# Ten more matmuls of zeros ahead of two groups of transposes in an attention and MLP kernel

## The chip, the cores and the metric

The kernel runs on one core of a Trainium2 chip. The metric is the device time of one execution in microseconds; the time of a kernel is the median of several executions. A profile is one more execution, recorded instruction by instruction. Engines are named as in the profile: PE (TensorE's matmuls), PEld (its weight loads), DVE (VectorE), ACT (ScalarE), POOL (GpSimd) and SP (SyncE).

## The reference

For each of 8 batches there are 8 heads with 512 tokens `x` and 32 states `state`, 64 wide. Tokens read the states and states read the tokens with a softmax each way; the 544 rows of a batch, 512 wide over the heads, then go through a two-layer MLP of width 2048 with a leaky activation of its own slope per unit.

```python
scores = scale * np.matmul(x, state.transpose(0, 1, 3, 2))       # softmax over the 32 states
xread = np.matmul(a, state)
scores2 = scale * np.matmul(state, x.transpose(0, 1, 3, 2))      # softmax over the 512 tokens
sread = np.matmul(a2, x)
attn_out = np.concatenate([xread, sread], axis=2)
h = attn_out_rows @ w_in                                         # 4352 x 512 @ 512 x 2048
g = np.maximum(h, 0.0) + alpha * np.minimum(h, 0.0)
out = g @ w_out
```

## The kernel before

All work is cut into steps, and the text `ORDER` (from line 17) lists the steps of the whole kernel in the order in which they are issued. The loop over `ORDER` (line 799) splits each entry at the dots and calls the function of that name. An engine takes its instructions in that order and waits at each for what it needs; nothing is rearranged behind it. So for each engine the order in `ORDER` is the order of its queue.

The steps that matter around the change, for batch 0:

- `lx0`, `lst`, `wi`, `wo`, `lx`: transfers issued by POOL's queue. `lx0` (line 202) brings the second half of the heads of x, `lst` (line 218) the states of batches 1 to 7, `wi.0` (line 224) the first quarter of w_in. The first half of x and the states of batch 0 come by the queues of SP and ACT and are cast by `xc` and `stc`.
- `stt.0`, `sto`: transposes of the states of batch 0 on PE, into PSUM bank 0, and their copy by ACT.
- `xt.b.j.g.k` (line 308): four transposes on PE of 128x128 parts of x, for the half `g` of the heads, into bank `k`. `xo` (line 315) copies them to `xT`, on the engine that its last letter names. `xt.0.1.1.3` and `xt.0.0.1.4` read what `lx0` brought.
- `sc.0.0` and `sc.0.1` (line 318): the scores of the first and the second half of the heads, eight small matmuls each, into the double bank `two`. `sc.0` computes all sixteen again, for the softmax of the tokens.
- `sb.0.0`, `smax.0.0`, `ssh.p.0.0`, `sexp.0.0` and so on: the softmax of a half, on DVE, DVE, POOL and ACT.
- `str.i.k` (line 286): fourteen transposes on PE of half of the states that `lst` brought, into bank `k`; `sro` (line 291) copies them on ACT. `str.0.5` uses bank 5, `str.1.0` bank 0.
- `m.b.f.k0.k1`: the product of the states of batch `b` with a quarter `f` of w_in; `mo` casts it out of PSUM. `m.0.0.1.2` needs `wi.0`.
- `Z.k.n`: `zeros(k, n)` (line 240), `n` matmuls of a constant tile of zeros with itself into bank `k`. Nothing reads what they write. Before the change there are 76 of them, all in the first 17 us.

`single(k, ...)` (line 157) takes bank `k` of PSUM; a step that writes a bank waits until the one before has been written and read.

Of the kernel before, what the change touches and what calls it, by code (L numbers as in the profile page):

```python
# [15 lines left out]

ORDER = """
lx0 id lst stc xc.1.v xc.0.a oma wi.0 lx.1 Z.1.20 stt.0 Z.2.9 xt.0.1.0.1 xt.0.0.0.2 xo.0.1.0.v
xo.0.0.0.v sto.a Z.0.7 sc.0.0 xt.0.1.1.3 xt.0.0.1.4 str.0.5 sb.0.0 xo.0.0.1.v xo.0.1.1.a Z.1.4
sc.0.1 smax.0.0 str.1.0 sro.0.a wi.1 sb.0.1 wo.0 smax.0.1 wi.2 ssh.p.0.0 sro.1.a sexp.0.0 Z.1.3 sc.0  # L20
m.0.0.1.2 ssh.p.0.1 mo.0.0.a.0 Z.5.5 m.1.0.3.4 m.2.0.5.0 tm.0 mo.2.0.a.0 ssum.0.0 sexp.0.1
mo.1.0.a.0 mo.2.0.a.1 wo.1 Z.1.12 m.3.0.1.5 Z.3.7 xt.1.1.0.3 snorm.p.0.0 mo.1.0.v.1 te.0.1
# [809 lines left out]
```

## Time and profile before

| | us |
|---|---|
| median of three runs | 209.64 |
| lowest and highest of the three | 209.15, 209.68 |
| the profiled execution | 209.78 |
| its span, from the first to the last instruction | 208.0 |

| engine | busy us | share of the span | instructions |
|---|---|---|---|
| PE | 200.0 | 96% | 2028 |
| DVE | 175.3 | 84% | 273 |
| ACT | 145.5 | 70% | 291 |
| POOL | 181.0 | 87% | 119 |

Times in the timelines count from the start of the span. A timeline row has the start, the length of the merged group, the engine, the line, the operation, the tile written and the tiles read, the count, and in brackets the idle time of the engine before the group and what ended it. A matmul's length holds its way through the array, so matmuls overlap; how far apart they start is what they cost. The chain of waits is followed back from the last instruction: at each step to what released it, or to the instruction before it on its engine.

### The profile page before, as it was taken

The page shows a single profiled execution, that of the slowest core. Times are in us where ns is not written, and L with a number is a line of the kernel's source. Part 1 is how long each engine was busy: PE and PEld are TensorE (multiplying, and loading weights), DVE is VectorE, ACT ScalarE, POOL GpSimd, SP SyncE. Part 2 cuts the span into 40 slices and gives each one's busy share as a digit, 9 for nine tenths or more (in the row PEclk, how much of TensorE's full clock was granted, in tenths as well). Part 3 has the DMA queues.
Part 4 walks back from the last instruction along what each step waited for, and adds up shares of the span by engine and source line. Part 5 has one row for each costly group of instructions (what it writes and reads, how often), then busy time and mean ns, then how long its engine had stood idle before and what let it go on. Part 6 is the DMA issues. An engine that isn't in the chain of part 4 may idle for free.

```text
span 208.0 us, 5125 instructions
## 1 busy us (share of the span) xinstructions
PE 200.0 (96%) x2028; PEld 135.2 (65%) x2028; DVE 175.3 (84%) x273; ACT 145.5 (70%) x291; POOL 181.0 (87%) x119
## 2 busy tenths in 40 slices
PE   7789999999999999999999999999999999999993
PEld 6553344346557775766677776666678777888892
DVE  1797998999999999999999999998995997754331
ACT  4398996699998899988889579778654645451210
POOL 7569958999999999998999999979996972969960
PEclk9999999999999999999999999999999999999999
DMA  6999999799996749999995166035401144134143
GB/s 154 177 203 208 205 203 160 95 128 194 223 184 87 125 55 225 201 132 156 185 235 87 44 147 167 21 84 151 104 0 54 18 83 154 32 65 159 50 156 101
DMA packets 44792, 27.11 MB, mean 130 GB/s; under 512 B 22096, under 2 KB 42464, under 8 KB 44768
## 3 DMA queue, kind: packets, MB, share of 16 engines
q0 software_dynamic: 14192, 12.03, 38.3%
q1 hardware_dynamic: 29872, 14.23, 29.8%
q10 hardware_dynamic: 704, 0.52, 0.8%
q8 instruction: 16, 0.26, 0.5%
q14 instruction: 8, 0.07, 0.1%
HBM read 17.31 MB, written 8.91 MB: 126 GB/s over the span
## 4 chain that ended last, share of the span: by engine, by line
PE 71%; DVE 14%; ACT 5%; DMA 4%; POOL 4%; issue 2%; POOLq 0%
PE p L667 41%; PE h L518 19%; DVE gp L568 8%; DMA w_in_sb<-in_moe_w_in_dram 4%; PE h L527 3%; PE m_ps L485 3%; PE sr_ps L460 2%; ACT m L507 1%; DVE aT L396 1%; ACT neg L550 1%; DVE m L507 1%; POOL s L644 1%; ACT e L423 1%; POOL an L386 1%; PE o L587 1%
## 5 line engine op out<-in xcount | busy, mean ns | idle before, releaser
L550 ACT ACTIVATE neg<-h 128x512 f32<-128x512 f32 (+1 forms) x144 | 78.5, 583 | 27.4 <-PE h L518 18.5
L568 DVE SCALAR_TENSOR_TENSOR gp<-neg,oma_sb,h 128x512 f16<-128x512 f32 x128 | 89.0, 735 | 6.8 <-ACT neg L550 6.4
L518 PE MATMUL h<-aT,m 128*128 128x512 f16 x250 | 68.6, 379 | 0.3 <-DVE gp L568 0.3
L644 POOL TENSOR_TENSOR s<-gp,s 128x1024 f16<-128x1024 f16 x28 | 65.8, 2398 | 1.2 <-DVE gp L568 0.6
L667 PEld LDWEIGHTS <-gp 128*128 128x128 f16 x432 | 41.7, 98 | 13.9 <-issue 1.9
L667 PEld LDWEIGHTS <-s 128*128 128x128 f16 x368 | 35.2, 98 | 12.7 <-POOL s L644 1.7
L667 PE MATMUL p<-ws,s 128*128 128x256 f16 x248 | 37.3, 273 | 0.2 <-POOL s L644 0.2
L644 POOL TENSOR_TENSOR s<-gp 128x1024 f16<-128x1024 f16 x14 | 31.6, 2265 | 6.5 <-DVE gp L568 6.4
L518 PEld LDWEIGHTS <-m 128*128 128x128 f16 x250 | 23.6, 98 | 16.1 <-issue 3.3
L667 PE MATMUL p<-ws,gp 128*128 128x256 f16 x224 | 33.6, 273 | 0.0
L507 ACT CAST m<-m_ps 128x512 f16<-128x512 f32 x51 | 28.8, 599 | 4.8 <-PE m_ps L485 3.4
L667 PE MATMUL p<-w_out_sb,gp 128*128 128x256 f16 x208 | 30.6, 273 | 0.0
L370 POOL TENSOR_TENSOR ts<-ts,mx 128x1024 f32<-128x1024 f32 (+1 forms) x9 | 17.2, 1909 | 5.7 <-DVE mx L364 5.7
L667 PE MATMUL p<-w_out_sb,s 128*128 128x256 f16 x120 | 18.3, 273 | 0.0
L386 POOL TENSOR_TENSOR an<-ts,r 128x1024 f16<-128x1024 f32 (+1 forms) x9 | 16.3, 1810 | 1.8 <-DVE r L381 1.8
L587 PE MATMUL o<-w_out_sb,gp 128*128 128x512 f16 x64 | 16.6, 379 | 0.1
L620 POOL DMA_DIRECT2D gp<-gp x14 | 13.2, 967 | 3.5 <-issue 2.9
L568 DVE SCALAR_TENSOR_TENSOR gs<-neg,oma_sb,h 128x256 f16<-128x256 f32 x16 | 7.2, 478 | 8.2 <-ACT neg L550 8.2
L485 PE MATMUL m_ps<-w_in_sb,stT 64*32 64x512 f16 x256 | 11.7, 383 | 0.3
L587 PEld LDWEIGHTS <-gp 128*128 128x128 f16 x64 | 5.9, 97 | 8.1 <-issue 1.3
L423 ACT ACTIVATE e<-sc,nb 128x512 f16<-128x512 f32 x16 | 11.1, 694 | 0.1
L698 ACT COPY p<-p 128x512 f32<-128x512 f32 x11 | 6.5, 588 | 6.4 <-PE p L667 6.4
(76 smaller groups left out, 248.9 us busy)
## 6 DMA issues: line engine op xcount, KB each, us to landing
out_dram<-c SPq DMA_DIRECT2D x27, 256.0 KB, 3.1
xg<-in_x_dram POOLq DMA_DIRECT2D x7, 512.0 KB, 8.1
gp<-gp POOLq DMA_DIRECT2D x14, 256.0 KB, 3.6
w_in_sb<-in_moe_w_in_dram POOLq DMA_DIRECT2D x4, 512.0 KB, 11.8
w_out_sb<-in_moe_w_out_dram POOLq DMA_DIRECT2D x4, 512.0 KB, 13.1
out_dram<-osb SPq DMA_DIRECT2D x4, 256.0 KB, 4.4
out_dram<-c SPq DMA_DIRECT2D x3, 128.0 KB, 2.2
x<-in_x_dram SPq DMA_DIRECT2D x1, 256.0 KB, 3.3
```

The source lines that it names most:

```text
L370: engine(e).tensor_tensor(ts, ts, over_blocks(cols(live["mx", b], j, S // N)), ALU.subtract)
L386: engine(e).tensor_tensor(blocks(cols(live["an", b], j, S)), blocks(cols(live["ts", b], j, S)), over_blocks(cols(live["r1", b], j, S // N) ...
L423: nc.scalar.activation(live["e2", b][:, g, :, :], live["sc", b][:, :, :, g, :].rearrange("p r j s -> p (r j) s"), EXP, bias=live["nb", b][ ...
L485: nc.tensor.matmul(t[N * k : N * (k + 1), :], st_head(b, h)[64 * r : 64 * r + 64, :], w_in_sb[64 * r : 64 * r + 64, c, 512 * f : 512 * (f ...
L507: copier(e)(m_tile(b)[:, f, g, :], live["mp", b, f][g])
L518: nc.tensor.matmul(h.rearrange("p (r j s) -> p r j s", r=2, j=2), ms[b][:, f, g, 128 * j : 128 * (j + 1)], weights(b, g), start=(g == 0), ...
L550: nc.scalar.activation(neg, h, RELU, bias=0.0, scale=-1.0)
L568: nc.vector.scalar_tensor_tensor(gt, negs.pop((b, jc)), oma_sb[:, jc : jc + 1], h, ALU.mult, ALU.add)
L587: nc.tensor.matmul(outs[b, q], token_cols(b, jc, q), w_out_sb[:, jc, :], start=(jc == 0), stop=(jc == n_jc - 1),)
L620: nc.gpsimd.dma_start(gp[:, 1, 0], gp[:, 1, 1], accum_op=ALU.add)
L644: engine(e).tensor_tensor(t, x, y, op)
L667: nc.tensor.matmul(chains[chain][:, t, :], lhs, rhs[:, i, :], start=(opens and i == 0 and t == 0), stop=(i == half_k - 1), skip_group_chec ...
```

## The change

Two entries are put into `ORDER`. `Z.0.6`, six matmuls of zeros into bank 0, stands behind `sc.0.0` and ahead of `xt.0.1.1.3`. `Z.0.4`, four of them, stands behind `xt.0.0.1.4` and ahead of `str.0.5`. The order of all other steps is kept.

```diff
 lx0 id lst stc xc.1.v xc.0.a oma wi.0 lx.1 Z.1.20 stt.0 Z.2.9 xt.0.1.0.1 xt.0.0.0.2 xo.0.1.0.v
-xo.0.0.0.v sto.a Z.0.7 sc.0.0 xt.0.1.1.3 xt.0.0.1.4 str.0.5 sb.0.0 xo.0.0.1.v xo.0.1.1.a Z.1.4
+xo.0.0.0.v sto.a Z.0.7 sc.0.0 Z.0.6 xt.0.1.1.3 xt.0.0.1.4 Z.0.4 str.0.5 sb.0.0 xo.0.0.1.v xo.0.1.1.a Z.1.4
 sc.0.1 smax.0.0 str.1.0 sro.0.a wi.1 sb.0.1 wo.0 smax.0.1 wi.2 ssh.p.0.0 sro.1.a sexp.0.0 Z.1.3 sc.0
```

## The prediction

> **What bounds the kernel now.** I read the page's first two parts, then the chain of waits over the first 62 us, then each engine's timeline around the two places where zeros are put.
>
> ```profile
> span 208.0 us, 5125 instructions
> ...
> PE 200.0 (96%) x2028; PEld 135.2 (65%) x2028; DVE 175.3 (84%) x273; ACT 145.5 (70%) x291; POOL 181.0 (87%) x119
> ...
> PEclk9999999999999999999999999999999999999999
> ```
>
> PE is busy 96% of the span, so ten more matmuls look like a cost. But that is a mean over stages. Both groups of zeros fall between 7 and 9 us, and what counts is what sets the end there. The chain of waits, from its window over the start (start us, us, what):
>
> ```profile
> 2.81 0.54 POOL st L219
> 3.35 7.87 DMA w_in_sb<-in_moe_w_in_dram
> 11.22 0.04 issue
> 11.27 0.41 PE m_ps L485 x8
> 11.68 0.39 PE z L244 x5
> 12.06 0.57 PE m_ps L485 x16
> 12.63 0.02 issue
> 12.65 0.59 ACT m L507
> ```
>
> From 3.35 to 11.22 us the end is set by one transfer, the first quarter of w_in. PE joins the chain only at 11.27, with the states' first products (m.0.0 of the order). Whatever PE does before that is free as long as it is ready by then. PE's timeline up to there (start us, us, engine, line, operation, tiles, count, idle time before and its releaser):
>
> ```profile
> 1.10 2.31 PE L244 MATMUL z<-zero 128*128 128x128 f16 x20 [1.10 <-DVE zero L238]
> ...
> 5.78 0.55 PE L244 MATMUL z<-zero 128*128 128x128 f16 x7
> 6.95 0.30 PE L325 MATMUL sc<-xT,stT 64*32 64x256 f16 x8 [0.61 <-DVE xT L316]
> 7.49 0.62 PE L311 MATMUL xT_ps<-ident,xg 128*128 128x128 f16 x8 [0.24 <-DMA xg<-in_x_dram]
> 8.72 0.58 PE L259 MATMUL st_ps<-ident,st 128*64 128x128 f16 x14 [0.61 <-DMA st<-in_state_dram]
> 9.23 0.40 PE L244 MATMUL z<-zero 128*128 128x128 f16 x4
> 9.56 0.30 PE L325 MATMUL sc<-xT,stT 64*32 64x256 f16 x8
> 9.79 0.58 PE L259 MATMUL st_ps<-ident,st 128*64 128x128 f16 x14
> 10.31 0.34 PE L244 MATMUL z<-zero 128*128 128x128 f16 x3
> 10.70 0.41 PE L325 MATMUL sc<-xT,stT 64*32 64x256 f16 x16
> 11.27 0.41 PE L485 MATMUL m_ps<-w_in_sb,stT 64*32 64x512 f16 x8
> ```
>
> The reader is to see two gaps. After the first half of the scores (6.95) PE waits 0.24 us for the second half of x; after those transposes (7.49) it waits 0.61 us for the states. The six zeros go into the first gap, the four into the second.
>
> The chain from the states to 11.27 runs with little rest (8.72, 9.56, the score blocks on DVE, 10.70). PE ends the full scores at 10.70 + 0.41 = 11.11 and starts the products at 11.27. So the spare time behind the states' transposes is only about 0.16 us, and a delay of the row at 8.72 beyond that would move the end.
>
> **The cost of one zero.** The zeros' own line gives the duration of one (ns, min/median/max):
>
> ```profile
> L244 PE MATMUL z<-zero x76: 216/219/314, 1.1 to 16.4; 128*128 128x128 f16 x76
> ...
> 12.58 0.83 PE L244 MATMUL z<-zero 128*128 128x128 f16 x12
> ```
>
> A duration holds the pipeline; what occupies PE is the spacing. At 1.10: (2.31 - 0.31)/19 = 0.105 us. At 12.58: (0.83 - 0.22)/11 = 0.055 us, and at 5.78 likewise (0.55 - 0.22)/6 = 0.055. So PE runs at half rate at first and at full rate from before 5.78 on. The page's clock row shows nine throughout and doesn't show this start; the spacing does.
>
> **The six zeros.** They read the constant zero tile and write bank 0, whose last writer is the seven zeros of 5.78, so they wait for no other engine. The eight scores of 6.95 take 0.30 us together, so their starts lie a few hundredths apart; I put the last at 6.98, and that of 9.56 at 9.58. How soon a different kind of matmul follows is seen at 9.56 to 9.79: the transposes start 0.21 us after the scores' last start. So the first zero starts at about 7.19 and the sixth at 7.19 + 5 x 0.055 = 7.47; the next matmul may start at 7.52. The transposes started at 7.49: late by 0.03 us. Bounds: 0 if the zeros follow the scores at once, and 0.10 if another 0.07 us goes into weight loads.
>
> Who waits for these transposes:
>
> ```profile
> 7.32 0.72 DVE L358 STREAM_TRANSPOSE ts<-sc 128x512 f32<-128x512 f32 x1 [0.42 <-PE sc L325]
> 7.92 0.59 ACT L316 COPY xT<-xT_ps 128x512 f16<-128x512 f16 x1 [3.02 <-PE xT_ps L311]
> 8.14 0.42 DVE L316 COPY xT<-xT_ps 128x512 f16<-128x512 f16 x1
> 8.48 0.68 DVE L364 TENSOR_REDUCE mx<-ts 128x16 f32<-128x512 f32 x1
> 9.25 1.05 POOL L370 TENSOR_TENSOR ts<-ts,mx 128x512 f32<-128x512 f32 x1 [2.00 <-DVE mx L364]
> 9.34 2.22 ACT L293 COPY stT<-st_ps 128x896 f16<-128x896 f16 x2 [0.84 <-PE st_ps L259]
> 9.94 0.72 DVE L358 STREAM_TRANSPOSE ts<-sc 128x512 f32<-128x512 f32 x1 [0.77 <-PE sc L325]
> 11.45 1.05 POOL L370 TENSOR_TENSOR ts<-ts,mx 128x512 f32<-128x512 f32 x1 [1.16 <-DVE mx L364]
> ```
>
> ACT's copy (7.92) is followed by an idle 0.84 us; DVE's copy and maximum (8.14, 8.48) by an idle 0.77; POOL's subtraction (9.25) by an idle 1.16. The second half of the scores (9.56) needs both copies, which end at 8.56 at the latest. A delay of 0.03 to 0.10 is swallowed at each place. The DVE transpose at 7.32 waits for the scores themselves, ahead of the zeros, and doesn't move. **Price: 0.00.**
>
> **The four zeros.** They stand behind the transposes, whose last (0.22 long like a zero, an estimate) starts at 7.49 + 0.62 - 0.22 = 7.89, or 7.92 with the delay. The nearest row for zeros behind transposes is 9.23: its last transpose starts at 8.72 + 0.58 - 0.22 = 9.08, so they follow by 0.15. First zero at 8.07, fourth at 8.07 + 3 x 0.055 = 8.24, PE free for the next at 8.29. With the delay at its bound (0.10) it is 8.36. The states' transposes start at 8.72, when their transfer has landed: 0.36 to 0.43 us to spare. **Price: 0.00.** If that cover were gone, because the states landed by 8.0, the loss would be 0.15 + 4 x 0.055 = 0.37, less the spare 0.16: 0.21 us.
>
> **Sum.** 0.00 + 0.00 on the profiled execution's own 209.78 us (span 208.0 and 1.78 around it), which stands 0.14 us above the median of 209.64. I forecast the median unchanged, 209.6. From the bounds: a loss of at most 0.21 us, and a gain of nothing, unless the clock gains, which is the first rival.
>
> **Rival 1, faster: the clock.** Zeros can matter only by keeping PE's clock up. The view by windows, over one stretch with the two gaps and over the end (PE busy with its count, then the other engines, granted clock, DMA share, GB/s):
>
> ```profile
> 5.58:9.00 3.42, 1.96 (x39) 1.51 (x38) 2.83 (x9) 0.59 (x1) 1.67 (x3) 1.00 1.10 175
> ...
> 203.55:206.96 3.41, 0.86 (x9) 0.54 (x7) 0.62 (x2) 0.37 (x1) 0.00 (x0) 1.00 0.48 154
> 206.97:208.00 1.03, 0.00 (x0) 0.00 (x0) 0.00 (x0) 0.00 (x0) 0.00 (x0) 0.50 0.00 0
> ```
>
> At the end, after 3.4 us with 0.86 us of PE work, the clock is at half. From 5.58 to 9.00, the sparsest early stretch, PE works 1.96 of 3.42 us and the clock stays up; the zeros at 9.23, spaced (0.40 - 0.22)/3 = 0.06, confirm it. So in this execution nothing was lost that zeros could save.
>
> [...]
>
> The price, if other executions do lose the clock behind 9.0: the chain's PE stretch from 11.27 to 12.63, 1.36 us, would take up to twice as long, so the change would save up to 1.36 us: 208.3. Against it: the profiled execution kept its clock and is no faster (209.78) than the median. At the most, the spread of the three runs (209.15 to 209.68) is the clock, and the change makes all like the lowest: 209.15, which is within 0.3%.
>
> **Rival 2, slower: zeros at half rate in front of the states.** If PE's clock comes up one step later in most executions, past 8.5 us, the zeros cost 0.105 each. The sixth starts at 7.19 + 5 x 0.105 = 7.72, the eight transposes run from 7.82 to a last start at 8.56, the four zeros from 8.71 to 9.03, and the states' transposes start at 9.13 instead of 8.72. That is 0.41 us, on a chain whose spare 0.16 is then gone: 210.05. With all ten zeros uncovered (both landings early as well) it would be 10 x 0.105 = 1.05 us: 210.7. It decides from the moment when PE is free for the states later than 8.88 (8.72 + 0.16). For it: the rate does change, only some 1.5 us ahead of the zeros. Against it: that is ahead of them, and the profiled time is typical.
>
> [...]
>
> **Rival 3: no effect because the zeros do nothing.** The clock is up already, so they change neither rate nor order; the result is that of the forecast, 209.6.
>
> **How the numbers follow.** No change (the forecast with rival 3, and the small ends of rivals 1 and 2): 0.66. Rival 1 beyond 0.3%: 0.15. Rival 2 beyond 0.3%, with any shift of a transfer's landing by the moved work: 0.19. About 0.3%, 0.63 us, is what a measurement of this kernel can tell from no change, so that is also the border of these cases: 209.0 and 210.3. The range reaches a little into both rivals: from 208.8, between 209.15 and 208.3, to 210.5, between 210.05 and 210.7. The likeliest case alone spans 209.15 to 209.85 (lowest run; median plus 0.21).
>
> **What would show it.** Right: the row of the second transposes starts within 0.1 us of 7.49 and the states' row at 8.72 still names the transfer as its releaser, with an idle time of some 0.3 us in place of 0.61; the chain still runs through w_in to about 11.2 and the products start within 0.1 us of it. Rival 1 would show as a time clearly below 209.0 with the clock lost somewhere in executions of the kernel before. Rival 2 would show as zeros spaced 0.1 us and the states' row released by PE itself. The prediction is wrong if the products of 11.27 move by more than 0.3 us, or if a difference appears behind 13 us with the start unchanged.

## The result, and the profile after

The changed kernel took 211.32 us in the median of six runs (211.06 to 216.56), against 209.41 us for the kernel before (208.85 to 209.79, six runs): a ratio of 1.0091, with a 95% interval from 1.0071 to 1.0111. It is slower by 0.9%. (The one execution of 216.56 had a mean clock of 0.992; it has no trace.) The prediction was 209.6 us with a range from 208.8 to 210.5 and called it "no change".

The page after the change: the span, PE, and the queue by which instructions are brought (packets, MB, share of 16 engines).

```profile
span 209.3 us, 5145 instructions
...
PE 201.3 (96%) x2038; PEld 136.2 (65%) x2038; DVE 175.4 (84%) x273; ACT 145.5 (70%) x291; POOL 181.0 (86%) x119
...
q8 instruction: 16, 0.26, 0.5%
```

PE has ten matmuls and ten weight loads more and 1.3 us more busy time. The instruction queue looks harmless at 0.5% of the engines. It has the same 16 packets as before the change, and it turns out to be the row that matters.

First the place where the zeros were put. PE's timeline of the changed kernel:

```profile
5.93 0.95 PE L244 MATMUL z<-zero 128*128 128x128 f16 x7
6.94 0.42 PE L325 MATMUL sc<-xT,stT 64*32 64x256 f16 x8
7.29 0.51 PE L244 MATMUL z<-zero 128*128 128x128 f16 x6
7.63 0.61 PE L311 MATMUL xT_ps<-ident,xg 128*128 128x128 f16 x8
8.08 0.39 PE L244 MATMUL z<-zero 128*128 128x128 f16 x4
8.61 0.58 PE L259 MATMUL st_ps<-ident,st 128*64 128x128 f16 x14
...
11.16 0.41 PE L485 MATMUL m_ps<-w_in_sb,stT 64*32 64x512 f16 x8
```

Here nearly all is as forecast: the second transposes start 0.14 us later than before (7.63 for 7.49), the states' transposes and the products not later but 0.11 us earlier (8.61 for 8.72, 11.16 for 11.27). The states landed that much earlier in this execution. Behind the zeros the states' weight loads still waited 0.32 us for them, where they had waited 0.79 us before:

```profile
8.61 0.42 PEld L259 LDWEIGHTS <-st 128*64 128x64 f16 x14 [0.32 <-DMA st<-in_state_dram]
```

One thing differs ahead of the change. The seven zeros at 5.93 are spaced (0.95 - 0.31)/6 = 0.107 us, so PE still ran at half rate there (the six behind the scores are 0.058 us apart). The trace's first record of the full granted clock is at 7.23 us; in the trace of the kernel before it is at 5.59 us.

Matched instruction by instruction, PE stays 0.11 to 0.13 us ahead of the kernel before from 8.6 us to 63.1 us. Then come these rows. PE's timeline before the change:

```profile
62.92 1.03 PE L518 MATMUL h<-aT,m 128*128 128x512 f16 x4
63.79 0.60 PE L667 MATMUL p<-ws,gp 128*128 128x256 f16 x4
```

and after it:

```profile
62.79 1.03 PE L518 MATMUL h<-aT,m 128*128 128x512 f16 x4
65.08 0.61 PE L667 MATMUL p<-ws,gp 128*128 128x256 f16 x4 [1.25 <-DMA gp<-gp]
```

Up to 62.79 the changed kernel is ahead by 0.13 us; then PE waits 1.25 us for a transfer, and from there to the end it is 1.29 us behind, with no further step. The difference of the two profiled executions (211.06 - 209.78 = 1.28 us) comes from this one wait. (The medians lie 1.91 us apart: 209.78 is at the upper end of the executions before, 211.06 the lowest of those after. What the other 0.6 us is stays open; beside the same kernel before, two of the experiments below with the same wait came out 1.2 and 1.3 us above it.)

The transfer is the second one of batch 1 by which POOL's queue adds one half of `gp` to the other (`A.1.1.1.d`, line 620). The chain of waits over this stretch, before:

```profile
58.12 0.04 issue
58.16 1.22 POOL gp L620
59.38 2.17 POOL s L644
61.56 0.05 issue
61.60 1.48 PE p L667 x12
63.09 0.86 PE h L518 x4
63.95 1.75 PE p L667 x16
```

and after:

```profile
58.01 0.04 issue
58.05 6.98 DMA gp<-gp
65.03 0.05 issue
65.08 1.92 PE p L667 x16
```

Before, the transfer is not on the chain at all; it took 5.1 us. After, it takes 6.98 us and is the chain. What held it up is seen in the DMA view of the changed kernel for 62.0 to 62.2 us (queue, kind: packets, MB, share of 16 engines):

```profile
q0 software_dynamic: 19, 0.04, 108.4%
q8 instruction: 1, 0.02, 44.6%
q1 hardware_dynamic: 9, 0.00, 5.8%
```

and in the same view of the kernel before, for 62.8 to 63.0 us:

```profile
q8 instruction: 1, 0.02, 29.4%
q0 software_dynamic: 3, 0.00, 1.9%
```

The instruction queue (q8) brings 16 pieces of 16384 B, one packet each. The records don't name the engine whose instructions they are; I read them as PE's (matmuls and weight loads, 4076 of them, where ACT as the next has 291). In 16 pieces that is 255 for each on average, so by this reading, with more instructions ahead, a piece is due earlier in the program. (By their start times the fetches are less even: in this run 168 to 327 PE instructions begin between one fetch and the next.) Before, the fifth piece starts at 62.86 us, when the adding transfer (q0) is down to its last small closing packets. After, it starts at 62.08, in the middle of it. The packets of both queues, from the trace's DMA records:

```
changed kernel                           start us   length ns
q8  16384 B                              62.081     1426
q0   2048 B  (15 engines' last one)      62.888      178
q0   2048 B  (six more, one by one)      63.491, 63.664, 63.870, 64.079, 64.290, 64.473
```

Fifteen engines are done at 63.05. The fetch ends at 62.08 + 1.43 = 63.51, and at 63.49 one engine begins on six packets that it still owes; it is done at 64.63. The records do not name the engine of a packet; that it is the one with the fetch is read from these two times. In the six's run and in that with ten zeros elsewhere, below, the remaining packets likewise begin at the fetch's end (63.04 for 63.05, 63.73 for 63.75). So, by this reading, the one engine that carried the instructions finished its share of the transfer 1.58 us after the others, and PE's products had to wait for it.

The theory tested below (F, the fetch): twenty more instructions in PE's stream, wherever they stand ahead of that point, bring the fetch forward into the transfer. Its rival (S): the loss comes from the places where the zeros stand, by an early step, the clock or a shift in the order of the early work.

### The profile page after: what moved, and what is told of

It is laid out like the page before. It is cut to its first block, busy times and chain, and to the rows that moved or that the text cites. A ratio compares the mean times of both kernels' runs of the same rounds, so it can differ in the third digit from the quotient of the medians.

```text
span 209.3 us, 5145 instructions
## 1 busy us (share of the span) xinstructions
PE 201.3 (96%) x2038; PEld 136.2 (65%) x2038; DVE 175.4 (84%) x273; ACT 145.5 (70%) x291; POOL 181.0 (86%) x119
## 4 chain that ended last, share of the span: by engine, by line
PE 69%; DVE 14%; DMA 7%; ACT 5%; POOL 2%; issue 2%; POOLq 0%
PE p L667 40%; PE h L518 18%; DVE gp L568 8%; DMA w_in_sb<-in_moe_w_in_dram 4%; PE h L527 3%; DMA gp<-gp 3%; PE m_ps L485 3%; PE sr_ps L460 2%; ACT m L507 1%; DVE aT L396 1%; ACT neg L550 1%; DVE m L507 1%; ACT e L423 1%; POOL an L386 1%; PE o L587 1%
## 5 line engine op out<-in xcount | busy, mean ns | idle before, releaser
L644 POOL TENSOR_TENSOR s<-gp 128x1024 f16<-128x1024 f16 x14 | 31.1, 2227 | 6.5 <-DVE gp L568 6.3
```

The costliest lines, as they stand in the source:

```text
L644: engine(e).tensor_tensor(t, x, y, op)
```

## The experiments

Each edit is one of the text `ORDER`. In all, the kernel before ran again beside them; its medians were 209.83 (31 executions, first group), 209.64 (21, second) and 209.72 (22, third).

### Only the four zeros, only the six

```diff
 against the changed kernel, first and second
-Z.0.7 sc.0.0 Z.0.6 xt.0.1.1.3 xt.0.0.1.4 Z.0.4 str.0.5
+Z.0.7 sc.0.0 xt.0.1.1.3 xt.0.0.1.4 Z.0.4 str.0.5
+Z.0.7 sc.0.0 Z.0.6 xt.0.1.1.3 xt.0.0.1.4 str.0.5
```

> Only the four zeros ahead of the states' transposes. Theory F (fetch): PE's instructions come by transfers of 16 KB; twenty more instructions ahead of the fifth fetch moved it from 62.86 to 62.08 us, into the second accumulating transfer (A.1.1.1.d), and the one DMA engine that carried it finished its share 1.6 us late. Eight more instructions should move that fetch by about 8/20 of 0.8 us, to about 62.5, still ahead of the transfer's end at 62.9: the products of 63.8 late by some 0.7 to 1.2 us, 210.1 to 210.9 us. Theory S (six): the cause is where the six zeros stand, behind the scores; without them 209.4.

> Only the six zeros behind the scores. Theory F: twelve more instructions, fetch at about 62.4, products late by some 0.8 to 1.3 us, 210.2 to 211.3 us. Theory S: the whole loss, 211.3.

The four: 209.82 us, ratio 0.9987 (0.9948 to 1.0026), no wait for the transfer. The six: 211.04 us, ratio 1.0056 (1.0024 to 1.0088). PE's timeline of the run with the six:

```profile
64.72 0.61 PE L667 MATMUL p<-ws,gp 128*128 128x256 f16 x4 [1.31 <-DMA gp<-gp]
```

Theory F missed on the four: it had a loss in proportion, and there was none. The piece is not brought in step with the count; with eight instructions it still came behind the transfer (64.67 in an execution that ran 1.5 us late as a whole, its clock at half from 8.80 to 12.21; right behind the transfer's last packet at 64.53), with twelve it came at 61.38, in the middle, where 62.4 was expected. These two runs alone would also fit S, that the six are to blame. The next two tell them apart.

### The same ten zeros elsewhere, and the ten paid back

```diff
 against the kernel before
-sto.a Z.0.7 sc.0.0
+sto.a Z.0.17 sc.0.0
 against the changed kernel
-wo.1 Z.1.12 m.3.0.1.5
+wo.1 Z.1.2 m.3.0.1.5
```

> The ten zeros all stand with the seven ahead of the scores (Z.0.17) and none at the two places of the change. Theory F: the same twenty instructions ahead of the fetch, so the same loss, 211.3, with the fifth fetch near 62.1. Theory S, or any cause that lies at the two places: 209.4.

> The change's ten zeros at their places, and ten of the twelve zeros at 12.6 us left out, so that as many instructions as before the change stand ahead of everything from 13 us on. Theory F: fifth fetch back near 62.9, no wait for the accumulating transfer, 209.4. Theory S or a loss through the clock or the early order: 211.3.

Ten zeros with none at the two places: 211.14 us, ratio 1.0043 (1.0006 to 1.0079). PE's timeline, and the DMA view for 62.0 to 62.2 us:

```profile
65.24 0.61 PE L667 MATMUL p<-ws,gp 128*128 128x256 f16 x4 [1.24 <-DMA gp<-gp]
```

```profile
q0 software_dynamic: 18, 0.04, 102.4%
q8 instruction: 1, 0.02, 51.3%
```

The wait is 1.24 us, nearly the same, with the fetch again in the middle of the transfer: the place doesn't matter. With all ten at their places and ten others left out: 209.81 us, ratio 1.0014 (0.9985 to 1.0043), no wait, and in the DMA view for 62.8 to 63.0 us the fetch stands alone:

```profile
DMA packets 1, 0.02 MB, mean 82 GB/s; under 512 B 0, under 2 KB 0, under 8 KB 0
...
q8 instruction: 1, 0.02, 41.6%
```

(The medians with the six and with ten elsewhere lie 1.2 and 1.3 us above the kernel before.) So the loss goes with the number of PE instructions ahead of the fetch and not with where the zeros stand. S fell here.

### The transfer moved away from the fetch

```diff
 against the changed kernel, and against the kernel before
-F.2.4.1 xd.4 mo.3.2.a.0
+F.2.4.1 mo.3.2.a.0
-Q.1.u.a tt.2 F.2.1.3
+Q.1.u.a tt.2 xd.4 F.2.1.3
```

> The changed kernel, with the transposing transfer of batch 4 (xd.4) issued behind that of the token weights (tt.2) instead of ahead of the second accumulating transfer. Theory F: that transfer then runs from about 58.7 to 61 us, ahead of the fetch at 62.1, and the wait of 1.3 us at 63.8 is gone although all ten zeros are there. The scores of batch 4 at 69.5 may wait for xT instead, by 0 to 1 us, in this kernel and in its twin without the zeros alike: the two within 0.3% of each other, between 209.2 and 210.5. Theory S (the loss lies in the early steps or the clock): this one 1.5 to 1.9 us slower than its twin.

> The kernel before with the same move of xd.4: the twin of the run with the zeros. Theory F: same time as that one within 0.3%. Theory S: 1.5 to 1.9 us faster than it.

With the zeros 214.23 us (four executions), without them 215.63 (five). The move itself cost more than expected: the scores of batch 4 waited 3 us for `xT`, and both lost clock. Without the zeros five products behind that wait, from 74.88 us, took 1.18 us, where the kernel before has eight in 0.87; with the zeros the mean clock is 0.992, and the granted clock is 1.00 in the stretches from 5.5 to 8.9 and from 9.2 to 12.6 us. PE's timeline of the run with the zeros:

```profile
72.49 0.41 PE L325 MATMUL sc<-xT,stT 64*32 64x256 f16 x16 [2.99 <-DMA xT<-xg]
```

So the medians say little on the 0.9%. What F said of the place itself held: with all ten zeros in, the transfer's last packet started at 61.63, the fetch followed at 61.79, and the wait at 63.8 was gone (PE runs 0.12 to 0.13 us ahead of the kernel before from 20 us right up to 69 us). The twin without the zeros was expected to be equal or, by S, faster; it was 1.4 us slower. In its profile the clock was lost a second time, early on, and four of its five executions have a mean clock of 0.984, where all four with the zeros have 0.991 or 0.992. The fifth, with 0.992, took 214.47 us, 0.1% from the median with the zeros: like for like the two agree as F had it, in one execution. The view by windows of the run without the zeros:

```profile
5.80:9.20 3.40, 1.68 (x31) 1.23 (x31) 2.34 (x8) 0.59 (x1) 1.46 (x2) 1.00 1.04 157
9.20:12.60 3.40, 3.40 (x67) 2.27 (x66) 1.87 (x3) 1.87 (x2) 1.19 (x2) 0.50 1.38 199
12.60:16.00 3.40, 2.96 (x64) 1.96 (x49) 3.11 (x6) 3.36 (x8) 2.35 (x3) 1.00 1.27 206
```

This is the prediction's first rival in the flesh: after a sparse stretch from 5.8 to 9.2 the granted clock is 0.50 until 12.6, and the first adding transfer is issued 1.5 us late (56.9 for 55.4). More on that below.

### More zeros, and fewer

```diff
 against the changed kernel: twenty; thirty has the second edit too
-sto.a Z.0.7 sc.0.0
+sto.a Z.0.17 sc.0.0
-wo.1 Z.1.12 m.3.0.1.5
+wo.1 Z.1.22 m.3.0.1.5
 against the kernel before: fewer
-wo.1 Z.1.12 m.3.0.1.5
+wo.1 Z.1.2 m.3.0.1.5
```

> Twenty zeros: the change's ten and ten more with the seven ahead of the scores. Were there a price for each zero, the loss would be twice that of the change: 213.2. Theory F: forty more instructions move the fifth fetch ahead of PE's wait at 61.2, among the packets of xd.4; one engine is then about 1 us late there and less late at the accumulating transfer: a loss between 0 and the change's own, 209.4 to 211.3, with the fetch between 58.5 and 61.5.

> The kernel before with ten fewer of the zeros at 12.6 us (2 for 12). Theory F: the fifth fetch moves away from the transfer, behind 62.9, and nothing is lost: 209.4 within 0.3%. If zeros at that place keep the clock up, a loss of some 0.5 us or more with zeros and products spaced 0.1 us behind 13 us.

> Thirty zeros: those of the run with twenty, and ten more with the twelve at 12.6 us. Sixty more instructions ahead of the fifth fetch. Theory F: the fetch starts ahead of the second accumulating transfer's packets (before 61.2), and the wait at 63.8 is at most that with forty instructions, 0.68 us, or gone: 209.4 to 210.6. A price for each zero: three times the change's loss, 215.

Twenty zeros: 210.61 us, ratio 1.0031 (1.0004 to 1.0057), less than with ten. The time lies where F had it, the fetch does not: it was expected between 58.5 and 61.5, among the packets of `xd.4`, and came at 61.69, still in the accumulating transfer. That packet took 0.89 us where the changed kernel's took 1.43, and the wait was shorter. PE's timeline:

```profile
64.57 0.61 PE L667 MATMUL p<-ws,gp 128*128 128x256 f16 x4 [0.68 <-DMA gp<-gp]
```

Thirty zeros: 210.61 us, ratio 1.0015 (0.9986 to 1.0045). PE's timeline, and the DMA view for 60.8 to 61.0 us:

```profile
64.59 0.61 PE L667 MATMUL p<-ws,gp 128*128 128x256 f16 x4 [0.78 <-DMA gp<-gp]
```

```profile
q1 hardware_dynamic: 146, 0.04, 100.5%
q8 instruction: 1, 0.02, 29.3%
```

Ten fewer: 209.75 us, ratio 1.0009 (0.9981 to 1.0037), no wait, the fetch at 63.90. A price for each zero is refuted: with thirty the loss is no larger than with twenty, and with ten it is the largest. With thirty the fetch comes ahead of the transfer, as expected, among the packets of `xd.4` (q1); but the wait there, 0.78 us, was expected to be 0.68 at most. It is of another kind: all 16 engines started the transfer late (first packet at 62.78, in the changed kernel at 61.36) and all were done together at 64.1. Whether it was the fetch among the packets of `xd.4` that held back every engine was not tried.

The records of all profiled executions side by side (us; done: the engines' completion writes; extra: PE instructions ahead of the fetch, against the kernel before):

```
kernel             extra  fetch   transfer: first packet, 15 engines done, last done   PE waits
before                 0  62.86   61.14   62.86   62.88   -
paid back              0  62.89   60.96   62.69   62.71   -
paid back once more    0  64.96   63.28   64.93   64.96   -
xd.4 later, without    0  64.26   61.50   62.98   63.00   -
fewer                -20  63.90   60.79   62.53   62.55   -
four                  +8  64.67   62.92   64.67   64.68   -
six                  +12  61.38   60.85   62.50   64.31   1.31
changed kernel       +20  62.08   61.36   63.05   64.63   1.25
ten elsewhere        +20  62.11   61.46   63.21   64.84   1.24
xd.4 later, with     +20  61.79   59.84   61.34   61.79   -
twenty               +40  61.69   61.41   63.07   64.02   0.68
thirty               +60  60.93   62.78   64.10   64.11   0.78
```

In four of them (six, changed, ten elsewhere, twenty) the fetch starts between the transfer's first packet and the end of the other engines, and in these four one engine is 0.96 to 1.81 us behind the other fifteen. In the kernel before, with the four, with `xd.4` later and the zeros, and with the paid-back version once more, the fetch starts within 0.02 us of the transfer's end. With `xd.4` later and the zeros one engine is 0.45 us behind the others although the fetch comes only after its packets, so a late engine is not by itself the mark of a fetch.

Counted in the program and not in time, the fetch keeps its place. Leave out the extra instructions and count the PE instructions that begin ahead of the fifth fetch: 1211 to 1217 in the four runs with none extra, 1195 to 1201 in the three with twenty, 1231 with twenty fewer; but 1215 with eight and 1195 with twelve, a step and not a slope.

### The paid-back version once more

> The ten zeros at their places, with ten fewer at 12.6 us, once more and against more runs. Theory F: the same as before within 0.3%, 209.5. Eight of 31 executions of the kernel before had shown a mean granted clock of 0.992 or less, at 210.6 us and above, and none of ten of this one. If the zeros keep the clock from falling behind 9 us, as the first rival of the prediction has it, again no more than one execution in sixteen shows that here, and the best version is this one by its upper half, not by its median.

209.89 us against 209.72, ratio 0.9982 (0.9953 to 1.0010). Of its 23 executions in two groups, one had a mean clock of 0.992 or less; of the kernel before, 12 of 74 had (8 of 31, 1 of 21 and 3 of 22). The one that lost it was this run's profile:

```profile
4.09:7.50 3.41, 1.60 (x23) 1.25 (x22) 1.77 (x8) 0.64 (x2) 3.16 (x5) 1.00 1.14 144
7.50:10.90 3.40, 3.14 (x40) 2.67 (x39) 1.94 (x4) 0.59 (x1) 0.00 (x0) 0.50 1.25 197
10.90:14.30 3.40, 3.09 (x78) 1.85 (x75) 2.53 (x3) 3.18 (x5) 2.13 (x3) 1.00 1.37 204
```

There the sparse stretch lay ahead of the added zeros (the first transposes waited 1.35 us for a cast of x). One of 13 here is also more than the one in sixteen that was expected. 1 of 23 against 12 of 74 would speak for a use of the zeros, but the other versions with all ten at these places don't bear it out: the changed kernel has 1 of 6, twenty 2 of 11, thirty 1 of 11, so that with the 1 of 23 it is 5 of 51. (A mean clock doesn't say where it was lost.) No version's median lies below that of the kernel before by more than 0.02 us.

## Why the prediction was wrong, point by point

- **What bounds the start** was right: the products started 0.11 us earlier than before, the transfer of w_in still ahead of them on the chain.
- **The spacing of the zeros** was right: six in (0.51 - 0.22)/5 = 0.058 us each. They followed the scores somewhat later than worked out (7.29 for 7.19): the scores, begun at 6.94 ahead of the full clock, took 0.42 us where they had taken 0.30. So the transposes were late by 0.14 us, above the bound of 0.10; it was swallowed, as argued.
- **The sum** is the step that failed: "0.00 + 0.00", with "a loss of at most 0.21 us". It counted what the zeros occupy on PE and who waits for them, and left out that they are also twenty instructions, which must be brought in. The term put at nothing is the fetch's: a packet of 1.43 us at 62.08 us, a wait of 1.25 us at 63.8. Its size hangs on where the fetch falls: with other counts the wait was nothing to 1.31 us.
- **"The zeros do nothing"**, the third rival, had them change "neither rate nor order". They changed the order of packets 55 us later: six of the transfer's stood behind a fetch that began at 62.08 us.
- **Rival 2** forecast the right sign by the wrong mechanism: no zero ran at half rate in the changed kernel's gaps (spacing 0.058), and the states' transposes were not late (8.61 for 8.72). The clock did come up later than before, as it supposed (7.23 for 5.59 us), but still 0.06 us ahead of the first zero. Its chance took in "any shift of a transfer's landing", which is near to what came, but without a place or a price. (Its 210.05 adds the full 0.41 us, where the price of the four zeros had taken off the spare 0.16.)
- **Rival 1** was judged rightly for the profiled execution and wrongly as a whole. That "other executions do lose the clock behind 9.0" is shown above in the profiles with `xd.4` later and without the zeros, and with the four; the mean clock of 12 of 74 executions of the kernel before, 0.992 or less, is in keeping with it. It doesn't touch the median. That so sparse a stretch keeps the clock was judged from one, with 1.96 of 3.42 us of PE work; the last section has three with 1.60 to 1.69 us that went the other way.
- **What would prove it wrong** was named: "a difference appears behind 13 us with the start unchanged". That is what came.

The page's row of q8 (16 packets, 0.26 MB; in the DMA records 16384 B each) was at hand before the prediction, and it was not read against the change. How an engine chooses between its queues no run shows. What the records show is that the transfer's last six packets, 0.18 to 0.30 us each, begin at 63.49 us, where the single packet of 1.43 us ends (63.51).

## What to carry to other kernels

An instruction that fills an idle gap for nothing is still an instruction: when one is added or taken out, later fetches of that engine's code can move (here, with twenty more, the fifth from 62.86 to 62.08 us), so look in the DMA view at each fetch (here 16 in 208 us) and at what transfer with little slack it may meet. If a small edit makes a difference far behind its place, match the two traces instruction by instruction for the first step, then look at the packets of the transfer that is late: one engine behind fifteen, its remaining packets beginning where a fetch ends, is the sign (here 1.58 us behind, and 63.49 for 63.51). Paying back the count elsewhere, as many instructions out as in, is a cheap way to tell an edit's own effect from this one (here 209.81 us and no wait, with all ten zeros in).

## What the hardware showed that was not expected

- One packet of 16 KB with instructions took 0.89 to 1.68 us in the fetches near 62 us. In the four runs where it began in the midst of the adding transfer, one of that transfer's 16 engines was done 0.96 to 1.81 us behind the other fifteen, and PE waited 0.68 to 1.31 us.
- The fetch doesn't move in proportion to the count: eight more instructions left it behind the transfer, twelve brought it to 61.38. PE waits for other engines at several places there (0.20 us at 61.5 for POOL), which may make such steps; that is a guess, and what sets off a fetch was not tried.
- PE's clock fell to half while PE was far from idle: behind stretches with 1.68 of 3.40 us of PE work (`xd.4` later, without the zeros), 1.69 of 3.42 (the four) and 1.60 of 3.41 (paid back once more) the granted clock is 0.50 for the next 3.4 us; behind 1.96 of 3.42 us (before, 5.58 to 9.00) it stayed at 1.00. PE's busy time alone doesn't draw the line, as the view by windows shows for the four and then for the paid-back version near its end, where the clock stayed at 1.00 behind 1.66 of 3.42 us:

```profile
5.38:8.80 3.42, 1.69 (x31) 1.41 (x32) 2.16 (x7) 0.10 (x1) 1.87 (x3) 1.00 1.16 168
8.80:12.21 3.41, 3.34 (x49) 2.31 (x46) 1.92 (x4) 1.64 (x3) 1.05 (x1) 0.50 1.35 193
...
202.52:205.94 3.42, 1.66 (x17) 1.25 (x14) 0.90 (x3) 0.37 (x1) 0.00 (x0) 1.00 0.35 112
205.94:207.78 1.84, 0.00 (x0) 0.00 (x0) 0.00 (x0) 0.00 (x0) 0.00 (x0) 1.00 0.24 78
```

None of those 17 matmuls is a transpose. In the three stretches that lost the clock 0.79 to 1.00 us were transposes, in the one of the kernel before that kept it 1.26 us. What counts as work for the clock stays open.
